# Attention and SwiGLU block on one core: the first pair's query and key loads cut into halves on two queues

## The chip, the cores and the metric

The kernel runs on one core of a Trainium2 chip. The metric is device time of one execution in microseconds (us), lower is better. An execution has five instruction streams: PE (matrix products, with its weight loads shown as PEld), DVE (vector), ACT (scalar), POOL (GpSimd) and SP (which here only issues transfers). Each stream runs strictly in its own order; streams wait for one another, and for transfers, through semaphores.

## The reference, cut to what matters

Four batches, eight heads, 768 positions, head size 64. Three heads attend causally to everything, five only to the first four positions and a window of 64. The heads' outputs are put side by side and go through a gated feed-forward block.

```python
q, k, v: (4, 8, 768, 64) float32; w_gate, w_val: (512, 1536); w_out: (1536, 512)
scores = (q @ k^T) / 8                                   # per batch and head
mask   = causal if retrieval head (0, 2, 6) else causal & (key < 4 | q - key < 64)
a      = softmax(where(mask, scores, -1e9))
x      = (a @ v) -> (3072 tokens, 512)
out    = (silu(x @ w_gate) * (x @ w_val)) @ w_out        # (3072, 512) float32
```

## The kernel before

Queries and keys come in pairs of 128-row tiles: pair n holds 256 rows of one batch for all eight heads, 512 KB for the queries and as much for the keys. Pair 0 is the first work of the program. Each pair passes these steps:

- `load` issues the transfer of float32 data from DRAM to a buffer of the ring `raw` (11 buffers). Pair 0 (`n < XOLD`, XOLD is 1) is loaded by one transfer for the queries and one for the keys, both at line 354; pairs 1 to 4 by two halves each (line 349). All loads are issued by SP.
- `cast` turns `raw` into the float16 tile `hq`. For pairs 0 and 1 it is done in two halves of four heads. For pair 0, ACT casts both halves of the queries (q0) and the first half of the keys (k0) by `copy` (line 206); DVE casts the second half of the keys by `recast` (line 212).
- `transposes` (line 473) runs eight PE products that turn `hq` into PSUM, and `evac` copies them to `qT` and `kT`, which `scores` (line 567) reads. `exps` (line 579, ACT) follows, then `values` (line 597), `norm` (line 605), another transpose, and the feed-forward products `gate` (line 759) and output products (line 845).

The order of all this is written out by hand in three strings of digits (`ORDER`, `WAYS`, `SLOTS`): every engine's stream follows that order. At the start, PE has nothing to compute, so the order holds filler products (`warm`, line 321), whose results nobody reads: ten at the start, five behind the transposes of q0, four behind those of k0. Fillers are ordinary instructions, so PE doesn't pass them before they are done.

A layer below the kernel gives each transfer a completion semaphore, taken in turn from eight (`DMAHW0` to `DMAHW7`), and puts the needed waits ahead of the instructions. A transfer that takes a semaphore again first waits for the earlier transfer that had it. ACT needs one table load before its first instruction of the kind used here; it stands directly ahead of the first cast.

```python
T_iss[kd, n] = P.add(f"load {kd}{n}", ["SP"], (lambda kd=kd, n=n: load(kd, n)), takes=["raw"])
T_load[kd, n] = P.lands(T_iss[kd, n])
```

Of the kernel before, what the change touches and what calls it, by code (L numbers as in the profile page):

```python
# [119 lines left out]
def kernel(  # L120
# [13 lines left out]
    nc = tc.nc  # L134
# [50 lines left out]
    def buf(ring, shape, dt, name):  # L185
        if ring in ("gv", "o", "big"):
            at = DIGITS.index(running[-1].slots[ring])
            room = banks[:, at * 512:at * 512 + (1024 if ring == "big" else 512)]
            if dt == FH:
                room = room.bitcast(FH)  # L190
            count = 1
            for x in shape[1:]:
                count *= x
            room = room[:, 0:count]
            if len(shape) == 2:
                return room
            axes = "abcd"[:len(shape) - 1]
            return room.rearrange(f"p ({' '.join(axes)}) -> p {' '.join(axes)}",
                                  **dict(zip(axes, shape[1:])))
        return pools[ring].tile(shape, dt, name=name, tag=ring + running[-1].slots[ring])  # L200
# [9 lines left out]
    def recast(task, dst, src):  # L210
# [24 lines left out]
        out=ident, in_=ident, compare_op=ALU.not_equal, fill=1.0,  # L235
# [101 lines left out]
    XOLD = 1  # L337
# [3 lines left out]
    def load(kind, n):  # L341
        r = buf("raw", [128, 1024], FP, "raw")
        landed[kind, n] = r
        if kind in "qkx":
            b, pi = QP[n]
            sl = slice(pi * 256, (pi + 1) * 256)
            if kind != "x" and XOLD <= n < XPE:
                for s_ in range(2):
                    nc.sync.dma_start(
                        out=r[:, 512 * s_:512 * s_ + 512],  # L350
                        in_={"q": q, "k": k}[kind][b, 4 * s_:4 * s_ + 4, sl, :].rearrange(
                            "f (p j) d -> p f (j d)", j=8))
                return
            nc.sync.dma_start(
                out=r.rearrange("p (h x) -> p h x", h=H),
                in_={"q": q, "k": k, "x": v}[kind][b, :, sl, :].rearrange(
                    "h (p j) d -> p h (j d)", j=2))
        elif kind == "o":
            nc.sync.dma_start(
                out=r.rearrange("p (a n) -> p a n", a=2), in_=wod[:, 2 * n:2 * n + 2, :])  # L360
        else:
            nc.sync.dma_start(
                out=r.rearrange("p (a n) -> p a n", a=4),
                in_=(wgd if kind == "g" else wvd)[:, :, n * 256:(n + 1) * 256])

    T_load, T_iss = {}, {}
    for kd, n in ([(kd, n) for n in range(NP) for kd in "qkx"]
                  + [(kd, n) for kd in "gvo" for n in range(6)]):
        T_iss[kd, n] = P.add(f"load {kd}{n}", ["SP"], (lambda kd=kd, n=n: load(kd, n)),
                             takes=["raw"])  # L370
        T_load[kd, n] = P.lands(T_iss[kd, n])
# [381 lines left out]
    hs, gs, sg, sl, vs, o_open, o_sbs = {}, {}, {}, {}, {}, {}, {}  # L753
# [302 lines left out]
```

## Time and profile before

| | |
|---|---|
| time, median of 3 runs | 242.46 us (241.78 to 242.67) |
| the profiled execution: its time, its span | 242.79 us, 241.0 us |
| PE busy | 232.1 us, 96% of the span |
| DVE, ACT, POOL busy | 185.0, 146.0, 127.6 us |
| DMA, mean | 169 GB/s, with about 340 GB/s in the first third |

The span is the time from the first to the last instruction of the program; the time of an execution has a little around it (1.8 us here). The page also has the chain of work that ended last, which is followed back from the end: PE has 85% of it. A busy PE isn't a PE at full rate, since the records of its products overlap, and since the products of the first microseconds take longer.

### The profile page before, as it was taken

Reading aid. Unit: us, or ns where it says so; the run is one execution under the profiler, and the core shown is the slowest. Engines: PE = TensorE matmul, PEld = TensorE weight load, DVE = VectorE, ACT = ScalarE, POOL = GpSimd, SP = SyncE. Lnnn points to the kernel's source line nnn. Section 1 sums busy time; section 2 is a strip of 40 time slices with the busy share of each in tenths; the row PEclk is TensorE's granted clock in tenths of the full one; section 3 lists DMA queues with packets and bytes.
Section 4 is the critical chain, followed back from the end, with each engine's and each line's share of the span. In section 5 each row is a group of like instructions: output and inputs, shape, how many; then the busy total and the mean of one; then the engine's idle time right before and its main releaser. Section 6 shows DMA issues by size and latency. Waiting matters only on the chain.

```text
span 241.0 us, 5649 instructions
## 1 busy us (share of the span) xinstructions
PE 232.1 (96%) x2211; PEld 146.3 (61%) x2211; DVE 185.0 (77%) x344; ACT 146.0 (61%) x223; POOL 127.6 (53%) x144
## 2 busy tenths in 40 slices
PE   7999999999999998799999999999999999999993
PEld 2677865654566867455564466666746665467783
DVE  2679998989899985498946987568646897875984
ACT  3599999879888878659774684655761111421100
POOL 7395878563957402926969519598960020214220
PEclk9999999999999999999999999999999999999998
DMA  6999999999999979989887414202031000220224
GB/s 184 354 340 366 335 334 366 356 334 305 205 257 167 191 182 252 269 145 213 172 162 223 94 22 89 44 5 77 35 104 51 0 0 0 90 88 0 90 101 162
DMA packets 67179, 40.74 MB, mean 169 GB/s; under 512 B 25168, under 2 KB 61008, under 8 KB 67152
## 3 DMA queue, kind: packets, MB, share of 16 engines
q1 hardware_dynamic: 64832, 36.58, 60.9%
q10 hardware_dynamic: 2320, 3.80, 4.3%
q8 instruction: 17, 0.28, 0.5%
q14 instruction: 10, 0.08, 0.1%
HBM read 28.31 MB, written 6.29 MB: 144 GB/s over the span
## 4 chain that ended last, share of the span: by engine, by line
PE 85%; DVE 5%; DMA 3%; SPq 2%; ACT 1%; issue 1%; POOL 0%; DVEq 0%; POOLq 0%; ACTq 0%
PE banks L759 51%; PE banks L845 17%; PE banks L567 7%; PE banks L597 5%; DMA xt<-xb 3%; PE banks L321 3%; PE banks L473 2%; SPq L615 2%; ACT e L579 1%; DVE out_sb L866 1%; DVE h_sb L775 1%; DVE sil L769 1%; PE banks L621 1%; DVE xb L605 1%; DVE h_sb L826 0%
## 5 line engine op out<-in xcount | busy, mean ns | idle before, releaser
L765 ACT ACTIVATE sig<-banks 128x512 f32<-128x512 f32 (+1 forms) x76 | 42.4, 575 | 53.5 <-PE banks L759 45.9
L759 PE MATMUL banks<-xt,wg_sb 128*128 128x512 f16 (+1 forms) x304 | 71.0, 368 | 1.5 <-DMA xt<-xb 1.5
L759 PE MATMUL banks<-xt,wv_sb 128*128 128x512 f16 (+1 forms) x304 | 71.5, 368 | 0.0
L579 ACT ACTIVATE e<-banks 128x1024 f16<-128x1024 f32 (+2 forms) x68 | 60.0, 912 | 13.4 <-PE banks L567 8.9
L769 DVE SCALAR_TENSOR_TENSOR sil<-sig,banks 128x512 f32<-128x512 f32 (+1 forms) x76 | 48.8, 654 | 15.1 <-ACT sig L765 14.6
L775 DVE SCALAR_TENSOR_TENSOR h_sb<-sil,banks 128x512 f16<-128x512 f32 (+1 forms) x76 | 48.9, 655 | 11.0 <-PE banks L759 9.6
L587 POOL TENSOR_TENSOR e<-e,m 128x640 f16<-128x640 f16 (+1 forms) x22 | 38.0, 1729 | 26.7 <-ACT e L579 24.4
L845 PEld LDWEIGHTS <-h_sb 128*128 128x128 f16 x432 | 41.6, 98 | 9.4 <-DVE h_sb L826 0.2
L759 PEld LDWEIGHTS <-wg_sb 128*128 128x128 f16 x304 | 28.7, 98 | 28.5 <-DMA xt<-xb 1.8
L759 PEld LDWEIGHTS <-wv_sb 128*128 128x128 f16 x304 | 27.9, 98 | 26.8
L826 POOL TENSOR_TENSOR h_sb<-h_sb 128x768 f16<-128x768 f16 x14 | 22.9, 1640 | 31.2 <-DVE hs_sb L826 12.6
L866 DVE TENSOR_TENSOR out_sb<-banks,out_sb 128x512 f32<-128x512 f32 x41 | 27.8, 687 | 7.5 <-PE banks L845 5.8
L845 PE MATMUL banks<-wo_sb,h_sb 128*128 128x256 f16 x216 | 26.4, 273 | 0.0
L845 PE MATMUL banks<-wt_sb,h_sb 128*128 128x256 f16 x216 | 26.3, 273 | 0.0
L567 PE MATMUL banks<-qT,kT 64*128 64x128 f16 x472 | 20.3, 218 | 1.2 <-ACT qT L206 0.6
L567 PEld LDWEIGHTS <-kT 64*128 64x128 f16 x472 | 14.5, 94 | 11.0 <-issue 10.4
L597 PEld LDWEIGHTS <-e 128*128 128x128 f16 x472 | 17.5, 97 | 5.8 <-issue 1.3
L597 PE MATMUL banks<-vt,e 128*128 128x65 f16 x472 | 18.9, 193 | 0.9 <-ACT e L579 0.9
L206 ACT CAST hq<-raw 128x1024 f16<-128x1024 f32 (+1 forms) x17 | 15.9, 945 | 5.2 <-DMA raw<-in_q_dram 4.4
L826 POOL TENSOR_TENSOR hs_sb<-h_sb 128x768 f16<-128x768 f16 x5 | 8.2, 1639 | 20.0 <-DVE h_sb L775 20.0
L605 DVE TENSOR_TENSOR xb<-banks,rc 128x512 f16<-128x512 f32 x24 | 16.6, 691 | 1.8 <-DMA xt<-xb 1.0
L208 POOL CAST vt<-raw 64x512 f16<-64x512 f32 x22 | 13.4, 608 | 2.4 <-DMA raw<-in_v_dram 1.1
(58 smaller groups left out, 185.3 us busy)
## 6 DMA issues: line engine op xcount, KB each, us to landing
raw<-in_v_dram SPq DMA_DIRECT2D x12, 512.0 KB, 6.0
raw<-in_q_dram SPq DMA_DIRECT2D x8, 512.0 KB, 5.2
raw<-in_k_dram SPq DMA_DIRECT2D x8, 512.0 KB, 6.3
raw<-in_moe_w_gate_dram SPq DMA_DIRECT2D x6, 512.0 KB, 8.3
raw<-in_moe_w_val_dram SPq DMA_DIRECT2D x6, 512.0 KB, 8.5
raw<-in_moe_w_out_dram SPq DMA_DIRECT2D x6, 512.0 KB, 8.5
out_dram<-out_sb ACTq DMA_DIRECT2D x6, 512.0 KB, 2.8
raw<-in_q_dram SPq DMA_DIRECT2D x8, 256.0 KB, 6.4
```

The lines of the kernel that those rows point to most:

```text
L567: nc.tensor.matmul(sc[:, c:c + n, :], weights, moving, start=first, stop=last)
L579: nc.scalar.activation(out=to, in_=src, func=AF.Exp, scale=scale)
L587: ENG[task().way].tensor_tensor(out=ev, in0=ev, in1=mm, op=ALU.mult)
L597: nc.tensor.matmul(avs[t][:, odd, n * 66:n * 66 + 65], ee, vv, start=(m == 0), stop=(m == len(bl) - 1))
L605: nc.vector.tensor_tensor(out=xb.rearrange("p n o d -> p o n d"), in0=av[:, :, :, 0:64], in1=rc.to_broadcast([128, 2, 4, 64]), op=ALU.mult)
L759: nc.tensor.matmul(ps, wsb[:, kk, j * 128:(j + 1) * 128], xt[:, kk, c[0]:c[1]], start=(kk == 0), stop=(kk == 3))
L765: nc.scalar.activation(out=sg[g, j, c], in_=gs[g, j, c], func=AF.Tanh, scale=0.5)
L769: nc.vector.scalar_tensor_tensor(out=sl[g, j, c], in0=sg.pop((g, j, c)), scalar=1.0, op0=ALU.add, in1=gs.pop((g, j, c)), op1=ALU.mult)
L775: nc.vector.scalar_tensor_tensor(out=hs[g, j][:, c[0]:c[1]], in0=sl.pop((g, j, c)), scalar=0.5, op0=ALU.mult, in1=vs.pop((g, j, c)), op1=A ...
L826: ENG[T_hs[g, x][part].way].tensor_tensor(out=to, in0=a, in1=b, op=op)
L845: nc.tensor.matmul(room[:, n], left[:, j, 128 * x:128 * x + 128], right[:, j], start=(j == 0), stop=(j == NK - 1))
L866: nc.vector.tensor_tensor(out=cell(*to), in0=rooms[g, p], in1=cell(*other), op=ALU.add)
```

## The change

For pair 0 the single transfer of the queries becomes two of four heads each, one issued by SP and one by ACT, and the same is done for the keys. The places of the two loads in the written order, their buffers, the casts and everything behind them stay as they were.

```diff
         if kind in "qkx":
             b, pi = QP[n]
             sl = slice(pi * 256, (pi + 1) * 256)
+            if kind != "x" and n < XOLD:
+                for s_, eng in enumerate((nc.sync, nc.scalar)):
+                    eng.dma_start(
+                        out=r[:, 512 * s_:512 * s_ + 512].rearrange("p (h x) -> p h x", h=4),
+                        in_={"q": q, "k": k}[kind][b, 4 * s_:4 * s_ + 4, sl, :].rearrange(
+                            "h (p j) d -> p h (j d)", j=2))
+                return
             if kind != "x" and XOLD <= n < XPE:
                 for s_ in range(2):
                     nc.sync.dma_start(
```

The first instructions of ACT before, where the numbers behind names tell buffers apart (`raw_111` is the buffer of q0, `raw_115` that of k0, `raw_142` that of pair 1's queries) and `waits` names the semaphores that ACT waits for ahead of the instruction:

```order
L206 ACT_TABLE_LOAD
L206 CAST hq_171<-raw_111 128x2x4x64 [waits DMAHW0_49]
L206 CAST hq_171<-raw_111 128x2x4x64
L206 CAST hq_187<-raw_115 128x2x4x64 [waits DMAHW1_49]
L206 CAST hq_204<-raw_142 128x512 [waits DMAHW2_49,DMAHW3_49,PE_49,Activation_49]
```

The same place now, with k0 in `raw_116` and pair 1's queries in `raw_144`; the four halves have the first four semaphores, in the order q0 on SP, q0 on ACT, k0 on SP, k0 on ACT:

```order
L349 DMA raw_111<-in_q_dram 128x4x128
L349 DMA raw_116<-in_k_dram 128x4x128
L206 ACT_TABLE_LOAD [waits DMAHW1_49]
L206 CAST hq_173<-raw_111 128x2x4x64 [waits DMAHW0_49]
L206 CAST hq_173<-raw_111 128x2x4x64
L206 CAST hq_189<-raw_116 128x2x4x64 [waits DMAHW3_49,DMAHW2_49]
L206 CAST hq_206<-raw_144 128x512 [waits DMAHW4_49,DMAHW5_49,PE_49,Activation_49]
```

Two transfers stand at the head of ACT's stream, and the first cast now needs two semaphores; the wait for one of them (the half of q0 that ACT issues) stands ahead of the table load, which had no wait before.

The first transfers of SP before (`raw_148` is the buffer of pair 0's values, `raw_168` and `raw_190` those of pair 2's keys and queries):

```order
L354 DMA raw_111<-in_q_dram 128x8x128
L354 DMA raw_115<-in_k_dram 128x8x128
L349 DMA raw_142<-in_q_dram 128x1x512 x2
L349 DMA raw_145<-in_k_dram 128x1x512 x2
L354 DMA raw_148<-in_v_dram 128x8x128
L349 DMA raw_168<-in_k_dram 128x1x512
L349 DMA raw_168<-in_k_dram 128x1x512 [waits DMAHW0_49]
L349 DMA raw_190<-in_q_dram 128x1x512 [waits DMAHW1_49]
L349 DMA raw_190<-in_q_dram 128x1x512 [waits DMAHW2_49]
```

And now, where those three buffers are `raw_150`, `raw_170` and `raw_192`:

```order
L349 DMA raw_111<-in_q_dram 128x4x128
L349 DMA raw_116<-in_k_dram 128x4x128
L356 DMA raw_144<-in_q_dram 128x1x512 x2
L356 DMA raw_147<-in_k_dram 128x1x512 x2
L361 DMA raw_150<-in_v_dram 128x8x128 [waits DMAHW0_49]
L356 DMA raw_170<-in_k_dram 128x1x512 [waits DMAHW1_49]
L356 DMA raw_170<-in_k_dram 128x1x512 [waits DMAHW2_49]
L356 DMA raw_192<-in_q_dram 128x1x512 [waits DMAHW3_49]
L356 DMA raw_192<-in_q_dram 128x1x512 [waits DMAHW4_49]
```

SP issues as many transfers as before, in the same order, the first two at half the size. Since there are two transfers more in all, semaphores are used again two places sooner: the values of pair 0 and the first half of pair 2's keys have a wait that they had not, and the three transfers behind them wait for other ones.

## The prediction

> **What bounds the kernel now.** I read the page first, then PE's waits over the whole run, then the chain of work at the start, then the streams of ACT and SP there. The page's busy shares and its chain by engine:
>
> ```profile
> PE 232.1 (96%) x2211; PEld 146.3 (61%) x2211; DVE 185.0 (77%) x344; ACT 146.0 (61%) x223; POOL 127.6 (53%) x144
> ...
> PE 85%; DVE 5%; DMA 3%; SPq 2%; ACT 1%; issue 1%; POOL 0%; DVEq 0%; POOLq 0%; ACTq 0%
> ```
>
> PE's waits from 9 us to 240 us (who waits, for whom, us in total, times, longest):
>
> ```profile
> PE banks L759 <- DMA xt<-xb: 1.5, 1, 1.5
> PE banks L597 <- ACT e L579: 0.9, 1, 0.9
> PE banks L567 <- ACT qT L206: 0.6, 1, 0.6
> PE banks L567 <- DVE xb L605: 0.6, 1, 0.6
> ```
>
> PE waits only 3.6 us in 231 us, never for a load (`raw`), and each time for a product of its own earlier work that went through ACT, DVE or a transposing transfer. So what makes PE late in the first microseconds arrives at the end; I give no discount. The largest wait, 1.5 us, could absorb some if the transfer queue, not PE, set it; I count that in the range only.
>
> The chain at the start (start us, length us, what):
>
> ```profile
> 1.37 4.45 PE banks L321 x10
> 5.82 1.05 PE banks L473 x8
> 6.87 1.40 PE banks L321 x5
> 8.27 0.45 PE banks L473 x8
> 8.71 0.86 PE banks L321 x4
> 9.58 0.45 PE banks L473 x8
> ```
>
> PE's stream is without a hole: ten fillers, transposes of q0, five fillers, transposes of k0, four fillers, transposes of the next queries. See also the rate: ten fillers took 4.45 us (0.445 each), the last four 0.86 (0.215); eight transposes took 1.05, later 0.45. PE ran at half rate first. With t at 0.445 and the rest at 0.215, the middle five give t/0.445 + (1.40 - t)/0.215 = 5, t = 0.63: the rate doubled at about 7.5 us (6.87 + 0.63, to 0.1).
>
> ACT's stream at the start, and then PE's weight loads for the transposes of q0 (in brackets: idle time before, and who ended it):
>
> ```profile
> 0.74 1.28 ACT L206 ACT_TABLE_LOAD   x1 [0.74 <-PEq L1037]
> 5.07 1.14 ACT L206 CAST hq<-raw 128x512 f16<-128x512 f32 x2 [3.04 <-DMA raw<-in_q_dram]
> 6.85 0.62 ACT L206 CAST hq<-raw 128x512 f16<-128x512 f32 x1 [0.65 <-DMA raw<-in_k_dram]
> 8.29 0.62 ACT L206 CAST hq<-raw 128x512 f16<-128x512 f32 x1 [0.81 <-DMA raw<-in_q_dram]
> ```
>
> ```profile
> 5.74 0.34 PEld L473 LDWEIGHTS <-hq 128*128 128x128 f16 x4 [0.82 <-ACT hq L206]
> 6.25 0.34 PEld L473 LDWEIGHTS <-hq 128*128 128x128 f16 x4 [0.18 <-ACT hq L206]
> ```
>
> The table load takes 1.28 us while ACT has nothing else to do, and is over at 2.02. The cast of q0 starts when q0 lands, and PE starts the transposes 0.67 us later, at 5.74, nearly at the moment its tenth filler ends. Two things thus end together there: fillers and cast. An earlier landing finds PE in its fillers; a later cast finds PE waiting.
>
> **The change part by part.** *The table load.* As the order shows, it now stands behind the wait for ACT's half of q0, so its 1.28 us no longer lie in the 3.04 us of idle time but between the landing and the first cast. If the landing stays, the first cast starts at 5.07 + 1.28 = 6.35 and the transposes at 5.74 + 1.28 = 7.02. This is the largest certain term.
>
> *The landing.* The transfers of q0 and of k0 (KB, us to landing), and then busy time, PEclk, DMA share and GB/s by stretches:
>
> ```profile
> raw<-in_q_dram SPq DMA_DIRECT2D x1, 512.0 KB, 4.3
> ```
>
> ```profile
> raw<-in_k_dram SPq DMA_DIRECT2D x1, 512.0 KB, 5.6
> ```
>
> ```profile
> 0.56:3.97 3.41, 2.60 (x7) 0.95 (x8) 0.00 (x0) 1.28 (x1) 2.80 (x10) 1.00 0.48 139
> 3.97:7.38 3.41, 3.41 (x15) 1.44 (x14) 1.84 (x8) 1.67 (x3) 2.13 (x8) 1.00 1.14 332
> 7.39:10.80 3.41, 3.41 (x38) 2.18 (x37) 1.86 (x5) 1.67 (x4) 1.23 (x2) 1.00 1.12 338
> 236.10:239.40 3.30, 1.22 (x12) 0.85 (x9) 2.00 (x4) 0.00 (x0) 0.00 (x0) 1.00 0.68 225
> 239.50:241.00 1.50, 0.00 (x0) 0.00 (x0) 0.00 (x0) 0.00 (x0) 0.00 (x0) 0.50 0.03 9
> ```
>
> q0 landed 4.3 us after its issue at 0.74, k0 5.6 after 1.26 (5.04 and 6.86). The trace shows no pair of halves on two queues, so I bound it. Best: by 3.97 the engines had moved 139 x 3.41 = 474 KB, which at 332 GB/s takes 1.43 us; were they at full rate from the end of q0's issue (1.19), q0 would land 3.97 - 1.19 - 1.43 = 1.35 us earlier. Worst: ACT's half of q0 travels behind SP's half of k0, half the distance from 5.04 to 6.86, 0.9 us later. I take 0: the same bytes go in the same order, q0's halves at the head of both queues, and from 3.97 on the engines are full (share 1.14). [...]
>
> *ACT's two issues.* ACT issues transfers late in this program:
>
> ```profile
> L883 ACTq DMA_DIRECT2D out_dram<-out_sb x6: 378/378/418, 130.6 to 225.5; - x6
> ```
>
> Two of 0.38 to 0.42 us fill 0.74 to 1.6, hidden in the wait for q0 up to 5.04. Without that cover: 0.8 us.
>
> *SP's stream* (issue start, length):
>
> ```profile
> 0.74 0.45 SPq L354 DMA_DIRECT2D raw<-in_q_dram  x1
> 1.26 0.56 SPq L354 DMA_DIRECT2D raw<-in_k_dram  x1
> ...
> 5.31 0.59 SPq L354 DMA_DIRECT2D raw<-in_v_dram  x1
> 5.94 1.24 SPq L349 DMA_DIRECT2D raw<-in_k_dram  x2
> 7.22 1.25 SPq L349 DMA_DIRECT2D raw<-in_q_dram  x2
> ```
>
> The new waits are for q0's halves (5.04), ahead of issues that came at 5.31 and 5.94: nothing. The second half of pair 2's keys, issued at about 6.6, now waits for SP's half of k0 (6.86): up to 0.25 us for it and for all behind it on SP. This is covered by the backlog of the DMA engines (share 1.12 until 10.80); uncovered it costs 0.25.
>
> *PE.* ACT casts q0 until 7.49 and then k0's first half until 8.1; DVE's half stays at 6.85. PE has five fillers ahead of k0's transposes, so k0 is not the limit. PE's work is fixed, and it loses 1.28 us at 5.74. Until 7.5 it ran at half rate, so these are worth 0.64 us of full-rate work. If the rate doubles later than 7.5, each us of that costs another 0.5.
>
> *The clock term.* PE started at 1.37 and its rate doubled at 7.5, after 6.1 us of nearly unbroken work. Now a hole of about 1.4 us (5.6 to 7.02) stands in that stretch. Lower bound: the hole doesn't matter, the rate still doubles at 7.5, cost 0. In favour: 1.54 us of idle time later left the full rate alone, as four products of 512 columns in 1.02 us show:
>
> ```profile
> 98.11 1.02 PE L759 MATMUL banks<-xt,wg_sb 128*128 128x512 f16 x4 [1.54 <-DMA xt<-xb]
> ```
>
> Upper bound: the 6.1 us count anew from 7.02, the rate doubles at 13.1, cost 0.5 x 5.6 = 2.8. Against the lower bound: from 0.56 to 3.97 PE was idle for 0.81 us of 3.41 and no rise followed; with 0.25 us idle in the next 3.41 it did; the new hole is nearer to the first. So I take the middle, a rise at 10.3, cost 1.4. [...]
>
> *Sum*: 0.64 + 1.4 = 2.04 on the profiled execution's 242.79 (span 241.0 and 1.8 around it), 244.8. That execution was 0.33 above the median of the three runs; on the median, 242.46 + 2.04 = 244.5.
>
> **The rivals.** *The clock isn't lost.* The table load is late, but the rate doubles before the hole or in spite of it. If by 5.6, PE pays the whole 1.28 (243.7), since nothing runs at half rate any more; if at 7.5, 0.64 (243.1). For it: the 98.11 row. Against: that row is at full rate, and a hole may hinder a rise without causing a fall. [...]
>
> *No cost, on the other side.* The table load runs early after all, or q0 lands so early that it is made up. Then the cast is at 5.07 or before; the gain is capped, because PE is in its ten fillers until 5.6 and has five more behind: 5.74 - 5.6, and the 0.18 that the second weight loads waited, at most 0.3. Time 242.2 to 242.5. It decides once q0's landing plus 1.28 is under 5.04, a landing by 3.76, just the best bound above; or if the wait is not ahead of the table load on the chip. Against: the stream is in order, and the first bytes would have to come at full rate at once.
>
> *A later landing.* ACT's half is served behind k0's: 0.9 more, a hole until 7.92. PE loses 2.18, worth 1.09; the clock's middle moves to 10.75, cost 1.63; 242.46 + 2.72 = 245.2. For it: q0's first bytes crawl (139 GB/s). Against: ACT issues at 0.74 like SP.
>
> **How the numbers follow.** A run of this kernel can't tell less than 0.5% (1.2 us) from no change. Forecast 0.50; clock not lost 0.28; no cost 0.15; later landing 0.07. Slower by over 0.5%: 0.50 + 0.07 + 0.06 of the second case (its upper end) = 0.63. Within: 0.22 + 0.12 = 0.34. Faster: 0.03. The range goes from 243.0, under the second case, to 245.5, over the later landing and most of the clock term's upper part (all of it would be 242.46 + 0.64 + 2.8 = 245.9); outside are the no-cost case and that tip.
>
> **What would show it.** ACT's table load at about 5.0 instead of 0.74, directly ahead of the first cast; that cast at about 6.35; PE's weight loads of q0 with about 2.1 us of idle time before them, ended by ACT, instead of 0.82; fillers of 0.43 us behind them, and 0.215 only from about 10 us on; from 20 us on the same stream shifted by about 2 us with no new waits. I am wrong if the table load is at or before 2 us, if q0 lands well under 4.5, if the five fillers are at full rate by 7.5, or if PE's waits behind 60 us shrink.

## The result and the profile after

| | time, us | ratio to before (95%) |
|---|---|---|
| before, 20 runs | 242.34 (241.65 to 243.89) | |
| changed, 20 runs | 243.44 (242.03 to 245.14) | 1.0054 (1.0035 to 1.0072) |
| the profiled execution of the changed kernel | 244.32, span 242.5 | |

The changed kernel is 1.1 us slower. The 20 times also lie wider apart: their standard deviation is 0.77 us against 0.49; but in a later series (e5 to e8 below) the kernel before had 0.69, so the wider spread isn't sure. The profiled execution of e2 below took 1342 us, against 241.76 to 243.07 for the eleven others of its kernel, and is left out, as is one of the kernel before, of 608 us.

ACT's stream at the start of the changed kernel, from the timeline:

```profile
0.74 0.50 ACTq L349 DMA_DIRECT2D raw<-in_q_dram  x1
1.27 0.58 ACTq L349 DMA_DIRECT2D raw<-in_k_dram  x1
4.68 1.28 ACT L206 ACT_TABLE_LOAD   x1 [4.68 <-DMA raw<-in_q_dram]
5.97 1.66 ACT L206 CAST hq<-raw 128x512 f16<-128x512 f32 x3
8.29 0.62 ACT L206 CAST hq<-raw 128x512 f16<-128x512 f32 x1 [0.66 <-DMA raw<-in_q_dram]
```

The table load has gone from 0.74 to 4.68, behind a wait for a transfer of q0, and the first cast from 5.07 to 5.97. PE's first weight loads of q0, and then the chain at the start:

```profile
6.64 0.34 PEld L480 LDWEIGHTS <-hq 128*128 128x128 f16 x4 [1.73 <-ACT hq L206]
```

```profile
0.74 3.86 DMA raw<-in_q_dram
...
4.68 1.28 ACT L206
5.96 0.01 issue
5.97 0.63 ACT hq L206
6.60 0.05 issue
6.64 1.13 PE banks L480 x8
7.77 2.13 PE banks L321 x5
9.90 0.85 PE banks L480 x8
10.76 0.94 PE banks L321 x4
11.70 0.45 PE banks L480 x8
```

Before, the chain there was PE alone, from 1.37 on. Now it runs over the transfer, the table load and the cast. The five fillers take 2.13 us (0.426 each) instead of 1.40, and the transposes of k0 0.85 instead of 0.45: PE's rate doubled at 10.79 us (from the trace's clock record, where it was 7.39 before), 3.41 us later; the expectations below call this length a window or a stretch. The transposes of the next queries come at 11.70 instead of 9.58, 2.12 us late. At the end 1.5 us of that is left. PE's waits from 9 us on:

```profile
PE banks L766 <- DMA xt<-xb: 1.7, 1, 1.7
PE banks L574 <- ACT qT L206: 0.6, 1, 0.6
PE banks L604 <- ACT e L586: 0.6, 1, 0.6
```

The 0.6 us that PE waited for DVE's `xb` is gone and the wait for ACT's `e` is 0.3 shorter.

### The profile page after: what moved, and what is told of

It is laid out like the page before. It is cut to its first block, busy times and chain, and to the rows that moved or that the text cites. A ratio compares the mean times of both kernels' runs of the same rounds, so it can differ in the third digit from the quotient of the medians.

```text
span 242.5 us, 5654 instructions
## 1 busy us (share of the span) xinstructions
PE 233.4 (96%) x2211; PEld 146.9 (61%) x2211; DVE 185.2 (76%) x344; ACT 145.9 (60%) x223; POOL 127.1 (52%) x144
## 4 chain that ended last, share of the span: by engine, by line
PE 90%; DMA 4%; DVE 3%; ACT 2%; issue 0%; DVEq 0%; ACTq 0%
PE banks L766 52%; PE banks L852 20%; PE banks L574 8%; PE banks L604 5%; PE banks L480 2%; DMA xt<-xb 2%; DMA raw<-in_q_dram 2%; PE banks L321 1%; ACT e L586 1%; DVE h_sb L833 1%; PE banks L628 1%; DVE out_sb L873 1%; ACT L206 1%; DVE e L594 0%; DVE xb L612 0%
```

## The experiments

Theory A: the loss comes from the table load behind the wait. Theory B: it comes from the second queue itself. Theory C: the hole in PE's stream (0.83 us in the profile after) makes the rate double later in some executions; theory D: the rate has nothing to do with it. Theory E: a late PE is partly made up between 60 and 98 us; theory F: it isn't. Each kernel was timed against the kernel before on the same chip.

| run | time, us | ratio (95%) |
|---|---|---|
| e1_table_first | 242.55 | 1.0009 (0.9992 to 1.0026) |
| e2_cast_by_load | 242.68 | 1.0010 (0.9993 to 1.0027) |
| e3_sp_only | 243.48 | 1.0049 (1.0025 to 1.0073) |
| e4_keys_only | 243.66 | 1.0054 (1.0035 to 1.0072) |
| e5_hole | 243.73 | 1.0037 (1.0017 to 1.0057) |
| e6_after_13 | 242.97 | 1.0015 (0.9994 to 1.0036) |
| e7_before_plus8 | 243.24 | 1.0036 (1.0011 to 1.0061) |
| e8_sp_halves_9 | 243.83 | 1.0054 (1.0033 to 1.0075) |

**The table load put first (e1).**

```diff
 # changed kernel, in load(), behind the two halves of pair 0
+                if kind == "k":
+                    nc.scalar.copy(out=first, in_=ident[:, 0:2])
```

> The changed kernel with one scalar copy of two columns of ident behind ACT's two loads, whose result nobody reads; it waits for one semaphore alone, so that the table load runs at about 1.9 us. Theory A (the table load, held back by the wait for a half of q0, and the clock that rises a window later because of the hole): first cast at about 5.07, PE's idle time before the transposes of q0 under 0.2 us more than before, time 242.2 to 242.5, ratio to before 0.999 to 1.001. Theory B (the second queue itself is what costs: slower transfers, later issues on SP): first cast late still, 243.2 to 243.6, ratio 1.004 to 1.006.

ACT's stream of this kernel:

```profile
1.88 1.28 ACT L355 ACT_TABLE_LOAD   x1 [1.88 <-issue]
3.18 0.19 ACT L355 COPY first<-ident 128x2 f16<-128x2 f16 x1
5.04 1.14 ACT L206 CAST hq<-raw 128x512 f16<-128x512 f32 x2 [1.67 <-DMA raw<-in_q_dram]
```

With the two queues kept and the table load early, the cast is at 5.04, and the time is that of before within the interval. A holds: the place of the table load is what costs. In this arrangement the second queue neither costs nor gives anything that can be measured (q0 is complete at 5.01 us, against 5.04 before).

**Casts cut as the loads are (e2).**

```diff
 # changed kernel, in cast()
+        if n < XOLD:
+            recast(T_c[n, kd, x],
+                   hqs[n, kd].rearrange("p k a (s d) -> p s (k a) d", s=2)[:, x],
+                   landed[kd, n].rearrange("p (s f d) -> p s f d", s=2, d=64)[:, x])
+            return
```

> The changed kernel with pair 0's casts cut along the halves of the loads, so that each cast needs one semaphore; then no wait stands ahead of the table load, without any added instruction. Theory A: table load at about 1.9 us, first cast at 4.65 when SP's half lands, second when ACT's half lands (5.07), transposes at 5.75; time 242.1 to 242.4, ratio 0.998 to 1.001. Theory B: 243.2 to 243.6.

Only the times of this run are used. They agree with e1, by another edit: with one semaphore for each cast, nothing stands ahead of the table load. The time is slightly above the expected range, which the interval covers.

**Both halves on SP (e3).**

```diff
-                for s_, eng in enumerate((nc.sync, nc.scalar)):
+                for s_, eng in enumerate((nc.sync, nc.sync)):
```

> The changed kernel with both halves of each load issued by SP, none by ACT; the first cast still needs two semaphores. Theory A: the table load waits for the half that is second in SP's queue, about 5.0, the cast starts at about 6.35, PE's hole is 0.4 us longer than in the changed kernel, time 243.4 to 244.2, ratio 1.004 to 1.008. Theory B: without a second queue there is no cost, 242.2 to 242.6, ratio 1.000.

```profile
4.63 1.28 ACT L206 ACT_TABLE_LOAD   x1 [4.63 <-DMA raw<-in_q_dram]
5.93 1.89 ACT L206 CAST hq<-raw 128x512 f16<-128x512 f32 x3
```

Without any second queue the loss is the same, and the table load is as late: two semaphores for the first cast are enough to hold it back. That the late table load is what costs here isn't shown, though: SP now issues two transfers more, what it loads behind them lands later (the first values at 12.01 instead of 11.34), and e8 below, with the same issues and an early table load, loses as much. I had the landing wrong: the halves were there at 3.72 and 4.56, not 5.0, so the cast is no later than in the changed kernel.

**Only the keys halved (e4).**

```diff
-            if kind != "x" and n < XOLD:
+            if kind == "k" and n < XOLD:
```

> Only the keys of pair 0 are halved on two queues, the queries are loaded by one transfer as before; the table load stands ahead of the first cast without a wait. Theory A: first cast at 5.07 to 5.2, transposes as before, 242.2 to 242.6, ratio 0.999 to 1.002. Theory B: about half of the loss of the changed kernel, 242.8 to 243.0, ratio 1.002 to 1.003.

```profile
1.28 1.28 ACT L206 ACT_TABLE_LOAD   x1 [1.28 <-PEq L1044]
5.94 1.66 ACT L206 CAST hq<-raw 128x512 f16<-128x512 f32 x3 [3.38 <-DMA raw<-in_q_dram]
```

A miss: the table load is early, as A said, and yet the time is that of the changed kernel, for another reason. ACT's half of k0 is issued at 0.74, together with the whole of q0 on SP, and lands 5.0 us later; q0 landed at 5.92 instead of 5.04. The cast is at 5.94, as late as the table load made it in the changed kernel, and by the medians the same lateness costs the same. So A is right about the changed kernel, but what sets the time is when the first cast of q0 is done; and here, other than in e1, a second queue did cost. (This profile is of the fastest of the twelve executions, 242.64 us.)

**A hole alone (e5).**

```diff
 # kernel before
-    def warm(n=10, at=None):
+    def warm(n=7, at=None):
```

> The kernel before with seven fillers at the start instead of ten: loads, casts and table load as before, but PE is idle from about 4.4 to 5.7 us, a hole as large as the late table load makes. Theory C (the rate doubles only after a busy stretch of 3.4 us whose place differs between executions, and a hole makes some executions miss one): time 0.6 to 1.5 us above before, 243.0 to 243.9, ratio 1.002 to 1.006, with a wider spread than before. Theory D (only the late cast costs; the rate of PE doesn't depend on the hole): 242.3 to 242.6, ratio 1.000, spread as before.

```profile
5.74 1.13 PE L473 MATMUL banks<-ident,hq 128*128 128x128 f16 x8 [1.20 <-ACT hq L206]
6.66 2.34 PE L321 MATMUL banks<-ident 128*128 128x512 f16 x5
```

Loads, table load and casts are those of before, and the transposes of q0 start at 5.74 as before. Only three fillers of no use are missing, and the kernel is slower by 0.37%: the five fillers behind the hole take 2.34 us instead of 1.61 in the same view, the rate doubled at 9.36. C holds in time and profile, D falls. The wider spread that C also expected didn't come: the standard deviation is 0.57 us, that of the kernel before in the same series 0.69.

**The hole filled (e6).** The same edit in the changed kernel, with 13 instead of 10.

> The changed kernel with 13 fillers at the start instead of ten, so that PE is busy until the late transposes of q0. Theory C: PE no longer misses a stretch; what is left is 0.6 to 0.9 us of PE's work, 242.9 to 243.2, ratio 1.002 to 1.003, with a spread like that of before. Theory D: fillers cannot help, and the last of them come a little later than the cast: 243.5 to 243.9, ratio 1.004 to 1.006.

```profile
6.55 0.92 PE L480 MATMUL banks<-ident,hq 128*128 128x128 f16 x8 [0.16 <-ACT hq L206]
7.30 1.24 PE L321 MATMUL banks<-ident 128*128 128x512 f16 x5
```

The table load is as late as in the changed kernel, but the loss is 0.15% instead of 0.54%. D's 0.4 to 0.6% lies outside the interval, C's 0.2 to 0.3% inside. So filling the hole gives something; since the intervals of the two kernels touch, how much isn't exact. That it is the clock which gains isn't shown by this profile: its rate doubled at 5.53, and two of three profiles of the changed kernel (r1 and r2 below) have their fillers at full rate too.

**PE late by a known amount (e7).** In the order of the kernel before, 12 fillers instead of four behind the transposes of k0.

```diff
-    "...0C1d1f0B2021y01g0g281e..."
+    "...0C1d1f0B2021y81g0g281e..."
```

> The kernel before with 12 fillers instead of four behind the transposes of k0, at full rate: PE, and nothing else, is 8 x 0.215 = 1.72 us later from about 10 us on. Theory E (transfers of the stretch from 60 to 98 us are late for PE anyway and take up about 1 us of a late PE): 0.6 to 1.0 us above before, ratio 1.002 to 1.004. Theory F (a late PE arrives at the end undiminished, as the prediction had it): 1.6 to 1.8 us, ratio 1.007.

The measured 0.36% is 0.87 us (0.27 to 1.48) for 1.72 us of fillers. F's 1.6 to 1.8 lies outside. So E holds by the times. Two products of line 845, before and then here:

```profile
83.09 1.47 PE L845 MATMUL banks<-wo_sb,h_sb 128*128 128x256 f16 x12
...
99.22 1.47 PE L845 MATMUL banks<-wt_sb,h_sb 128*128 128x256 f16 x12
```

```profile
84.85 1.47 PE L845 MATMUL banks<-wo_sb,h_sb 128*128 128x256 f16 x12
...
100.50 1.47 PE L845 MATMUL banks<-wt_sb,h_sb 128*128 128x256 f16 x12
```

PE is 1.76 us late at 83 us and 1.28 at 99. In the changed kernel the same two products start at 85.39 and 100.60: 2.30 late, then 1.38. But one pair of profiles doesn't size it. In e1 the same two products start at 83.26 and 97.56, 0.17 late and then 1.66 early, and from 103 us on it is 0.4 early, with nothing to make up. And this profile, whose rate doubled at 5.87 and not at 7.39, is only 1.23 us late at 10.81, where the next queries' transposes start. The size is known by the interval above alone, and where the delay is made up stays open.

**A version meant to beat both (e8).** The casts of e2, both halves on SP as in e3, nine fillers at the start.

> A version that may beat both: halves of q0 and k0 all issued by SP, casts cut along the halves (one semaphore each, table load early), and nine fillers at the start instead of ten. From the run with both halves on SP: halves of q0 at 3.7 and 4.6 us, so casts end at about 5.2, the transposes start at about 5.2 instead of 5.74. Theories A and C: 0.2 to 0.5 us less at PE, of which part arrives: 241.9 to 242.4, ratio 0.998 to 1.000. If the first microseconds don't matter: 242.4.

```profile
4.62 0.62 ACT L206 CAST hq<-raw 128x512 f16<-128x512 f32 x1 [0.22 <-DMA raw<-in_q_dram]
```

```profile
5.29 1.04 PE L485 MATMUL banks<-ident,hq 128*128 128x128 f16 x8
6.12 1.54 PE L321 MATMUL banks<-ident 128*128 128x512 f16 x5
8.12 0.61 PE L485 MATMUL banks<-ident,hq 128*128 128x128 f16 x8 [0.45 <-DVE hq L212]
```

A miss too: q0 is done early, but the time is up by 0.54%. SP now issues two transfers more, 0.45 to 0.51 us for each of its first four, and what it loads behind them lands later: the second half of k0 at 7.27 (k0 before: 6.83), the first values at 11.96 instead of 11.34. PE waits 0.45 us for that half of k0. In the changed kernel, where ACT takes those two issues, the values land at 11.34 as before. That the later landings are the whole loss of e8 is argued, not shown.

**The changed kernel again (r1, r2).** Two more profiles, unaltered.

> The changed kernel once more, unaltered, for another profile. Theory C: table load at about 4.6, cast at 5.95, transposes at 6.6 as in the first profile, but the doubling of PE's rate at another place: either between 4.8 and 6.2 (then PE's fillers behind the hole are at full rate and PE is 0.3 to 0.9 us behind the kernel before at 12 us) or later than 9.5 (then 1.5 to 2.1 us or more behind). If the place of the rise were fixed to the program: 10.8 again, and 2.1 us behind.

> As r1_changed_again, a third profile of the changed kernel; the same expectations, and if theory C holds the place of the rise differs among the three.

The chain of r1, and then of r2 (their lines are one number higher):

```profile
6.98 0.40 PE banks L481 x4
7.38 1.08 PE banks L322 x5
8.46 0.45 PE banks L481 x8
8.91 0.86 PE banks L322 x4
9.77 0.45 PE banks L481 x8
```

```profile
7.07 0.40 PE banks L481 x4
7.47 1.08 PE banks L322 x5
8.54 0.45 PE banks L481 x8
8.99 0.86 PE banks L322 x4
9.86 0.45 PE banks L481 x8
```

Table load and cast are late as in the first profile (4.50 and 5.79, 4.58 and 5.88), but here the five fillers behind the hole run at full rate (1.08 us) and the next transposes come at 9.77 and 9.86, 0.2 to 0.3 us behind the profile before, not 2.12 (the expectation said 0.3 to 0.9). The rate doubled at 5.16 and 6.25. These executions took 243.09 and 242.81; the first profiled one 244.32. C holds: the place of the rise differs among the three, and it decides how late PE is at 12 us.

It doesn't decide the whole time. First, the profile before had its rise at 7.39, so r1 and r2 are compared with a slower start. e7 is the kernel before up to the transposes of k0, with its rise at 5.87, and has them at 7.77 instead of 8.27:

```profile
7.77 0.45 PE banks L473 x8
```

Against that, r1 and r2 (8.46 and 8.54) are 0.69 and 0.77 us late, as much as their casts (5.79 and 5.88 against 5.10 in e7). Second, they lose more at 25 us. The kernel before, and then r1:

```profile
23.55 1.49 DVE L587 TENSOR_TENSOR e<-e,m 128x640 f16<-128x640 f16 x3
25.64 1.04 PE L759 MATMUL banks<-xt,wg_sb 128*128 128x256 f16 x8
```

```profile
23.75 2.33 DVE L595 TENSOR_TENSOR e<-e,m 128x640 f16<-128x640 f16 x3
24.38 1.15 POOL L209 CAST wv_sb<-raw 128x1024 f16<-128x1024 f32 x1 [1.82 <-DMA raw<-in_moe_w_val_dram]
26.46 1.03 PE L767 MATMUL banks<-xt,wg_sb 128*128 128x256 f16 x8 [0.46 <-DVE sil L777]
```

Three products of DVE take 0.84 us longer beside a cast on POOL, `sil` comes late, and PE waits for it. From 30 us on r1 is 1.06 and r2 1.16 us behind the profile before, and the first changed profile, which has no such wait, 2.36. e4 to e8 have the wait too. That POOL's cast holds DVE up is read from the overlap, not tested, and how often the kernel before meets it isn't on record.

## Why the prediction was right or wrong

The direction and the range held (243.44 in 243.0 to 245.5), the middle was too high: 2.04 us forecast, 1.1 measured. That the range held is in part luck: the lateness and what is left of it at the end were both taken too large, and 243.44 lies among the times of the rival "the clock isn't lost" (243.1 to 243.7) and not near the 244.5 of the forecast. Twenty runs gave 0.54% with an interval of 0.35 to 0.72, so this kernel can tell less than the 0.5% that the prediction named. By its steps:

- *The table load behind the wait*: right, and shown by e1. The size was off: 0.90 us of lateness (5.07 to 5.97; 0.72 and 0.81 in r1 and r2) instead of 1.28. The step that failed was which half is waited for: the first four semaphores go to ACT's half of q0, SP's half, ACT's half of k0, SP's half, not in the order that the part on the change gives. So the table load waited for SP's half, which landed at 4.60, and its last part covered the wait for ACT's (5.06).
- *The landing of all of q0, 0 us*: right for the pair (5.06 against 5.04). That the halves land 0.45 us apart I hadn't considered. In e1, too, the second queue left q0's landing where it was (5.01). In e8, where SP issues all the halves, the first values landed 0.62 us later (11.96 instead of 11.34).
- *ACT's issues, SP's new waits, 0 us*: right. ACT's issues took 0.50 and 0.58, hidden. The second half of pair 2's keys was issued 0.26 us later and landed at 12.70, as before.
- *PE's work, 0.64*: mis-sized with the lateness. In the first profile 0.90 at half rate is 0.45; in r1 and r2, with the early rise, PE pays the lateness whole, 0.7 to 0.8 (against e7).
- *The clock term, 1.4 us in every execution*: wrong in kind. It is paid in some executions and not in others. In the first profile the rise came at 10.79, 3.41 late, which costs 1.7 at half rate; in r1 and r2 it fell in front of the end of the hole and this term was nothing. There the rival "the clock isn't lost" was right, and with it one of the prediction's signs of being wrong: the five fillers ran at full rate by 7.5. The same 3.41 us separates the only two lengths from rise to fall that eleven profiles have, 232.11 and 235.52 us.
- *No discount on the way to the end*: wrong. e7 puts what arrives at about half of 1.72 us, and another sign of being wrong came with it: PE's waits behind 60 us shrank, from 3.0 us to 2.3 in the first changed profile. It was not the largest of them, for `DMA xt<-xb`, that gave way: it stayed at 1.6 to 1.7 us in e7, the first profile, r1 and r2 (1.5 before). The 0.6 us for `xb` went, in e1 too, where PE wasn't late. What takes the rest stays open.

The gain that the rival "no cost" capped at 0.3 us isn't there in e1 and e2 either; in e1 the first cast starts at 5.04, so there was no earlier q0 to gain from.

## What to carry to other kernels

The first cast here needed two semaphores and got a wait instruction of its own, and what was placed between the two, a one-off table load, left the time in which it was hidden: look at what stands between the wait and its user. Here the table load started 3.94 us later, and the first cast 0.90. A wait for one transfer is worth keeping as one, by cutting the consumer as the load is cut (e2: 0.10% slower instead of 0.54%). Where a core starts with fillers at half rate, as here, keep PE busy until the real work comes: a hole of 0.83 us was followed by 2.12 us of lateness in the first changed profile and one of 0.91 (r1) by 0.19 (0.69 against e7, whose rise was nearly as early), and one profile shows only one of the cases. Compare how late PE is at several places, and between profiles whose rise came at a like time: r1, whose PE was 0.19 us late at 9.77, had three products of DVE beside a cast of POOL at 23.75 (2.33 us instead of 1.49), and PE waited 0.46 us for what came behind them.

## What the runs showed of the hardware

- From rise to fall of PE's rate, the clock records have two lengths: 232.11 us in the kernel before, the first changed profile, e1 and e5, and 235.52 in r1, r2, e3, e4, e6, e7 and e8. They are 3.41 us apart, and about 68 and 69 times that. By PE's busy time in the profiles, 3.41 us without idle PE (before, 3.97 to 7.38, where the prediction has 0.25 of it) and 3.41 us with 0.43 of idle PE (r2, 2.84 to 6.25; 13%) were followed by the rise; 3.41 us with 0.81 (before, 0.56 to 3.97; 24%), with 0.83 (first changed profile, 3.97 to 7.38; 24%) and with 1.20 (e5, 2.53 to 5.94) were not.
- Three products of DVE took 1.49 us in the kernel before and 2.33 in r1, where one of them began while POOL cast `wv_sb`; in the kernel before the products were there first, and that cast took 1.36 us instead of 1.15.
- With a half transfer on ACT's queue issued at 0.74, in the same moment as the whole of q0 on SP's, q0 landed 0.88 us later than without it (5.92 in e4, 5.04 before).
- On SP, halves issued one after the other brought q0 in at 3.72 and 4.56, earlier than one whole transfer (5.04); the first values, which SP issued behind them, landed at 12.01 in e3 and 11.96 in e8 instead of 11.34.
